# A two-stage attention and expert kernel: every engine's instruction order written out in one table

## The chip, the cores and the metric

One core of one Trainium2 chip. The metric is the device time of the whole kernel in microseconds (us), the median of several runs. The core has a matrix engine (TensorE, PE in the profile), a vector engine (VectorE, DVE), a scalar engine (ScalarE, ACT), GpSimd (POOL) and SyncE (SP). Each engine works through its own list of instructions in order; an instruction waits on semaphores for what others have to finish first. SP and POOL issue nearly all DMA transfers.

## The reference

The first half is a linear recurrence with complex decay over 4 x 768 tokens, 8 heads of 48 channels; the second is four dense experts on its output, all of which every token passes:

```python
for t in range(S):                         # S = 768; the decay a is normalised, magnitude capped at 0.999
    S_re, S_im = ar * S_re - ai * S_im + k_t v_t^T, ar * S_im + ai * S_re
    y[:, :, t] = q_t @ S_re
x = y as 3072 rows of 384
for e in range(4):                         # w1[e] is 384 x 1024, w2[e] is 1024 x 384
    out += p[:, e:e + 1] * (np.maximum(x @ w1[e], 0.0) @ w2[e])      # p: domain_probs, each row divided by its sum
```

All in float32. The kernel writes a float32 operand as a high and a low part (`hi`/`lo`, `hh`/`hl`, `xh`/`xl`) and sums three products of them.

## The kernel before

**Stage 1** (to about 585 us) walks over 12 groups of 256 tokens. For a group `g`, `front()` (L806) makes the decay's running products on DVE and ACT (`norm`, `prefix` at L426 to L429 and L369 to L377, `head`, `tail`), and `attention()` (L706; `near_attention()`, L663, for the first two groups) runs two chunks of 128 tokens: transposes of K (`ktp`, `kp`), the state's increment (`dp`), scores (`sc`, masked on DVE into `scs`, L609) and values (`yp`, copied by ACT into `y`, L632). For the groups from 3 on, `y` goes to DRAM (`y_d`) and comes back transposed as `xa` (L218); groups 0 to 2 are turned on PE (`xp`, L656). ACT and DVE split the result into `xha` (L225) and `xla` (L227). Between these pieces runs `moe1()` on the group before, for experts 0 and 1, in eight steps `f2` per group: `w1_step` makes `ph` (L238), ACT cuts it at zero into `hh` (L249), DVE makes the rest `hl` (L250), and `w2_step` accumulates `po` (L261) from `hh` first and then `hl`. ACT scales `po` into `acc` (L743). `ph3_5` stands for group 3, step 5.

At the start, eight weight tiles are split with help of PE: `lp` (L206, L209), which ACT copies into `wlo` (L210). At the end of stage 1, `check_all()` (L751) reduces some statistics to one number (`n_ps` on PE, L765) and a `flag` (DVE, L766), which SP reads (L1477) to decide if a slower general path is run afterwards; and `late_weights()` (L768) sums weight tiles for stage 2 on DVE (`lws`, `lwt`, L779; `lwl`, `lwm`, L790) and stores them to DRAM (`late_d`, L793, L794). `lw28` is the last of three such batches.

**Stage 2** (to 955.8 us) runs experts 2 and 3 by a fast scheme of matrix products (`pb` and `pob`, L979) on blocks of 384 tokens. Its inputs `Z` are read back from `y_d` (L1118), added up on DVE and POOL (`Z<-Z`), and split into `xh` (ACT, L982) and `xl`. Its tiles take the SBUF space of stage 1, so that the first loads wait for stage 1's last stores. Its weights `shi`, `slo`, `ext` come from `late_d` (L1101, L1102) or from `w` through POOL (L1062, L1066).

The order on each engine is set by the framework's scheduler, which simulates the program, and by what pins it: `behind(ins, prev)` puts one instruction after another of its engine without a semaphore, `tc.keep_in_program_order` keeps an instruction behind the program's earlier ones, `WARM` puts the two last `lp` tiles of the start behind `qp` and `ktp`, and `NPIN` puts a group's scores behind a step of the experts.

Of the kernel before, what the change touches and what calls it, by code (L numbers as in the profile page):

```python
# [121 lines left out]

def fast_path(ctx, tc, qkP, aP, vP, probsP, w, out, flag):
# [1393 lines left out]
```

## Time and profile before

| | us |
|---|---|
| median of 3 runs | 966.08 (965.67 to 966.55) |
| the profiled execution | 963.93 |
| its span in the trace | 962.2 |
| PE busy in it | 935.6 (97%) |
| DVE, ACT, POOL busy | 740.6, 480.2, 165.2 |
| granted TensorE clock, mean | 0.997 of full speed |

The span is the time from the first to the last instruction of the trace; 1.7 us of the execution lie around it. A busy time counts the instructions of an engine; what is left of the span is the time that it waited. The page also names what ended each wait, and follows the chain of work that ended last.

### The profile page before, as it was taken

The numbers are of one execution on the slowest core, as the hardware profiler recorded it, in microseconds if no ns is written. First come the engines' busy times: TensorE is split into PE (matmuls) and PEld (weight loads), VectorE is DVE, ScalarE is ACT, GpSimd is POOL, SyncE is SP. The second block draws the span as 40 slices with busy tenths as digits, with TensorE's granted clock in tenths as the row PEclk, the third lists the DMA queues.
The fourth block names the chain that finished last, engine by engine and source line by source line (L and its number), as shares of the span: only waits on it lengthen the run. The fifth ranks groups of instructions, "written<-read, shape, count | busy, mean of one in ns | idle before, by whom it ended". The sixth has DMA issues, their size and how long they took to land.

```text
span 962.2 us, 18383 instructions
## 1 busy us (share of the span) xinstructions
PE 935.6 (97%) x7037; PEld 912.9 (95%) x7037; DVE 740.6 (77%) x1640; ACT 480.2 (50%) x952; POOL 165.2 (17%) x206
## 2 busy tenths in 40 slices
PE   5899999999999999999999999999999999999997
PEld 3799999989999999999999999999999999999997
DVE  7889989988989999889895676758485757676642
ACT  7756436364464636446253455636454554444430
POOL 6020000000000000000000026333534362322000
PEclk9999999999999999999999999999999999999999
DMA  9686175674857468393949799231514443131112
GB/s 299 193 156 165 54 202 137 166 150 135 179 149 187 120 149 192 113 216 97 215 115 275 268 302 273 60 116 41 151 60 137 155 96 99 50 99 50 50 50 77
DMA packets 131459, 139.57 MB, mean 145 GB/s; under 512 B 8802, under 2 KB 115090, under 8 KB 131362
## 3 DMA queue, kind: packets, MB, share of 16 engines
q1 hardware_dynamic: 116130, 107.84, 38.9%
q0 software_dynamic: 11488, 26.93, 12.1%
q10 hardware_dynamic: 3744, 3.54, 1.4%
q8 instruction: 57, 0.93, 0.4%
q14 instruction: 40, 0.33, 0.1%
HBM read 89.80 MB, written 48.47 MB: 144 GB/s over the span
## 4 chain that ended last, share of the span: by engine, by line
PE 60%; DMA 3%; DVE 2%; ACT 1%; issue 0%; SPq 0%; DVEq 0%; ACTq 0%
PE pob L979 20%; PE pb L979 17%; PE po L261 9%; PE ph L238 9%; PE sc L604 2%; PE yp L621 1%; PE yp L626 1%; DMA RX<-w 1%; PE dp L586 1%; DMA Z<-y_d 1%; PE ktp L567 1%; DMA late_d<-lwl 0%; DMA xa<-y_d 0%; DVE lws L779 0%; DMA y_d<-y 0%
## 5 line engine op out<-in xcount | busy, mean ns | idle before, releaser
L979 PE MATMUL pob<-shi,hid 128*128 128x384 f32 x528 | 148.3, 334 | 0.0
L261 PE MATMUL po<-whi,hh 128*128 128x384 f32 x384 | 129.9, 338 | 1.4 <-ACT hh L249 1.0
L261 PE MATMUL po<-wlo,hh 128*128 128x384 f32 x384 | 128.7, 335 | 0.0
L249 ACT ACTIVATE hh<-ph 128x512 fp32r<-128x512 f32 x96 | 57.1, 595 | 132.0 <-PE ph L238 126.2
L991 POOL TENSOR_TENSOR Z<-Z 128x384 f32<-128x384 f32 x84 | 90.6, 1123 | 112.3 <-DMA Z<-y_d 47.9
L238 PE MATMUL ph<-xha,whi 128*128 128x256 f32 x576 | 103.3, 287 | 2.9 <-ACT xha L225 2.8
L238 PE MATMUL ph<-xla,whi 128*128 128x256 f32 x576 | 101.8, 284 | 0.6 <-DVE xla L227 0.6
L238 PE MATMUL ph<-xha,wlo 128*128 128x256 f32 x576 | 102.4, 284 | 0.0
L979 PE MATMUL pb<-xh,shi 128*128 128x384 f32 x291 | 97.2, 335 | 0.6 <-DVE pb L985 0.6
L979 PEld LDWEIGHTS pob<-shi,hid 128*128 128x128 f32 x528 | 96.4, 188 | 0.2 <-DVE hid L988 0.2
L979 PE MATMUL pb<-xh,slo 128*128 128x384 f32 x288 | 96.2, 334 | 0.0
L979 PE MATMUL pb<-xl,shi 128*128 128x384 f32 x288 | 96.2, 334 | 0.0
L250 DVE SCALAR_TENSOR_TENSOR hl<-ph,hh 128x512 fp32r<-128x512 f32 x96 | 66.0, 688 | 32.3 <-ACT hh L249 31.8
L238 PEld LDWEIGHTS ph<-xha,whi 128*128 128x128 f32 x576 | 85.1, 190 | 5.4 <-ACT xha L225 4.0
L979 PE MATMUL pob<-slo,hid 128*128 128x384 f32 x264 | 88.2, 334 | 0.0
L261 PE MATMUL po<-whi,hl 128*128 128x384 f32 x384 | 84.3, 336 | 0.0
L238 PEld LDWEIGHTS ph<-xla,whi 128*128 128x128 f32 x576 | 83.2, 190 | 1.1 <-DVE xla L227 0.8
L238 PEld LDWEIGHTS ph<-xha,wlo 128*128 128x128 f32 x576 | 82.7, 190 | 0.2 <-issue 0.2
L982 ACT ACTIVATE SN<-pb 128x384 f32<-128x384 f32 x96 | 47.3, 492 | 66.6 <-PE pb L979 59.2
L985 DVE TENSOR_TENSOR xl<-Z,xh 128x384 fp32r<-128x384 f32 x104 | 60.1, 607 | 21.1 <-ACT xh L982 13.3
L261 PEld LDWEIGHTS po<-whi,hh 128*128 128x128 f32 x384 | 72.4, 189 | 2.2 <-ACT hh L249 1.4
L982 ACT ACTIVATE hid<-pb 128x384 fp32r<-128x384 f32 x76 | 37.3, 490 | 72.3 <-PE pb L979 71.7
(227 smaller groups left out, 2069.6 us busy)
## 6 DMA issues: line engine op xcount, KB each, us to landing
qk<-qkP SPq DMA_DIRECT2D x24, 384.0 KB, 3.6
acc_d<-acc POOLq DMA_DIRECT2D x24, 384.0 KB, 4.8
ACC<-acc_d SPq DMA_DIRECT2D x48, 192.0 KB, 2.9
A<-aP SPq DMA_DIRECT2D x22, 384.0 KB, 5.5
k_d<-K SPq DMA_DIRECT2D x40, 192.0 KB, 4.1
Kst<-k_d SPq DMA_DIRECT2D x40, 192.0 KB, 5.7
Z<-y_d SPq DMA_DIRECT2D x16, 384.0 KB, 3.9
q_d<-Q SPq DMA_DIRECT2D x24, 193.5 KB, 3.7
```

Of the source, the lines that this page charges most:

```text
L238: ins = nc.tensor.matmul(ph[:, u, :], wt[:, j * P:(j + 1) * P], xt[:, j, :], start=(n == 0), stop=(n == 3 * NJ - 1))
L249: wts["hh"] = nc.scalar.activation(hh, ph, AF.Relu)
L250: wts["hl"] = nc.vector.scalar_tensor_tensor(hl, ph, 0.0, hh, op0=ALU.max, op1=ALU.subtract)
L261: ins = nc.tensor.matmul(po[t], part[0][:, u, t * P:(t + 1) * P], wts[i][n][:, HD:], start=(i % FE == 0 and part[0] is hh and n == 0), sto ...
L567: ins = nc.tensor.transpose(kt_ps[:, j * P:(j + 1) * P], K[0][:, i, j * CG + c, :], ident)
L586: ins = nc.tensor.matmul(d_ps[o:o + n, h, :], KT[:, h, o:o + n], vc[:, h * D:(h + 1) * D], start=True, stop=True)
L604: ins = nc.tensor.matmul(s_ps[:, h, :], Kc[:, hf * 4 + h, :], Qc[:, hf * 4 + h, :], start=True, stop=True)
L621: ins = nc.tensor.matmul(yo, st[:, o:o + n], Qc[:, o // D, :], start=True, stop=False)
L979: return tc.keep_in_program_order(nc.tensor.matmul(*args, **kw))
L982: return pin(nc.scalar.activation(dst, src, fn, scale=scale))
L985: pin(nc.vector.tensor_tensor(dst, x, y, op=op))
L991: nc.gpsimd.tensor_tensor(dst, x, y, op=op)
```

## The change

The functions compute what they did, with the same instructions on each engine. `behind`, the arguments `prev` that carried its pins, `keep_in_program_order`, `WARM` and `pin` are dropped. A table `ORDER` lists, for each of five engines, runs of indices into that engine's instructions as the program writes them ("116+28" is 28 instructions from number 116 on). `pin_order`, called at the end of the fast path, ties each instruction of an engine to the one before it in the table, so that the scheduler has no choice left. The diff, cut to its core:

```diff
-WARM = {6: "pq", 7: "tk"}
-NPIN = 5
+NSOON = 6
+ORDER = {
+    "PE": (
+        "116+28 0+26 144+4 26+37 64+6 63 70+46 166+16 148+18 182+120 346+30 452+50 302+6 502+8 308+7 510+2 315+31 "
...
+def pin_order(tc, nc):
+    for name, table in ORDER.items():
+        own = [i for i in nc.cur_bb.bb.instructions
+               if i.engine.name == name and type(i).__name__ != "BassTilePoolBoundary"]
+        seq = []
+        for run in table.split():
+            at, _, n = run.partition("+")
+            seq += own[int(at):int(at) + int(n or 1)]
+        for prev, later in zip(seq, seq[1:]):
+            tc.add_manual_dep(later, prev.name,
+                              mybir.DependencyInfo(mybir.DependencyClass.NoSync, mybir.DependencyReason.DATA),
+                              reason="issue order")
...
-    def behind(ins, prev):
...
-                if g == 1:
-                    behind(ln, state["kt", 0, 1])
-                    behind(exp, state["kst", 0, 1])
...
-            if near:
-                wts["hold", g - 1, NF1 // 2 - 2] = ((5, state["sc", g, 1]),)
...
-                    ins = nc.vector.tensor_tensor(*o)
-                    if prev is not None:
-                        behind(ins, prev[1])
+                    nc.vector.tensor_tensor(*o)
...
         def pe(*args, **kw):
-            return tc.keep_in_program_order(nc.tensor.matmul(*args, **kw))
+            return nc.tensor.matmul(*args, **kw)
...
             fast_path(ctx, tc, qkP, aP, vP, probsP, w, out, flag)
+            pin_order(tc, tc.nc)
```

What it moves, at three places. In the rows below the second number of a name is the group (and step, chunk or half), the last one a running number.

**The start, ACT** (group 0, chunk 1). `KT`, `Kst` and `y` are copies that PE waits for; `s1` and `u1` belong to the preparation of group 1. Before:

```order
L568 ACTIVATE KT_156<-ktp0_1_1_408 128x8x48
L400 ACTIVATE s1_488<-s1_488,m2b_89 128x768
L577 ACTIVATE Kst_155<-kp0_1_0_420 112x4x128
L577 ACTIVATE Kst_155<-kp0_1_4_426 112x4x128
L401 ACTIVATE s1_488<-s1_488,lnb_85 128x768
L409 ACTIVATE u1_489<-s1_488 128x768
L411 ACTIVATE u1_489<-s1_488,neg1_83 128x768
L210 ACTIVATE wlo6_569<-lp6_0_571 128x384
L210 ACTIVATE wlo6_569<-lp6_1_575 128x384
L210 ACTIVATE wlo7_580<-lp7_0_582 128x384
L210 ACTIVATE wlo7_580<-lp7_1_586 128x384
L632 ACTIVATE y0_290<-yp0_0_446 112x4x128
```

And now:

```order
L559 ACTIVATE KT_156<-ktp0_1_1_408 128x8x48
L248 ACTIVATE wlo6_569<-lp6_0_571 128x384
L248 ACTIVATE wlo6_569<-lp6_1_575 128x384
L567 ACTIVATE Kst_155<-kp0_1_0_420 112x4x128
L567 ACTIVATE Kst_155<-kp0_1_4_426 112x4x128
L409 ACTIVATE s1_488<-s1_488,m2b_89 128x768
L410 ACTIVATE s1_488<-s1_488,lnb_85 128x768
L415 ACTIVATE u1_489<-s1_488 128x768
L417 ACTIVATE u1_489<-s1_488,neg1_83 128x768
L608 ACTIVATE y0_290<-yp0_0_446 112x4x128
L608 ACTIVATE y0_290<-yp0_1_456 112x4x128
L421 ACTIVATE u1_489,st_w_153<-u1_489,neg1_83 128x768
```

The two `Kst` copies no longer stand behind L400 (now L409), but behind two copies into `wlo6`; the `y` copies stand ahead of `wlo7` and of the last step of `u1`. On PE, the four `lp6` products now stand ahead of `qp`, and the first chunk-1 increment (`dp0_1`) ahead of the first `ph0_0`.

**The middle, PE and DVE.** On PE, before, the second half of group 3's values (`yp3_1`) stands behind the whole step `ph2_6`:

```order
L604 MATMUL sc3_1_1_2251<-Qst_154,Kst_155 128x128 x4
L238 MATMUL ph2_6_2382<-xha2_1826,wlo12_766 128x256 x3
L567 MATMUL ktp3_1_0_2258<-wide_76,K3_1851 128x128 x3
L238 MATMUL ph2_6_2382<-xla2_1827,whi12_600 128x256 x2
L567 MATMUL ktp3_1_1_2263<-wide_76,K3_1851 128x128 x3
L238 MATMUL ph2_6_2382<-xla2_1827,whi12_600 128x256
L238 MATMUL ph2_6_2382<-xha2_1826,whi13_602 128x256 x3
L238 MATMUL ph2_6_2382<-xha2_1826,wlo13_769 128x256 x3
L238 MATMUL ph2_6_2382<-xla2_1827,whi13_602 128x256 x2
L621 MATMUL yp3_1_2314<-Qst_154,G3_0_2238 48x128 x2
```

And now behind a part of `ph2_5` and three products of `po2_4`:

```order
L588 MATMUL sc3_1_1_2251<-Qst_154,Kst_155 128x128 x4
L558 MATMUL ktp3_1_0_2258<-wide_76,K3_1851 128x128 x3
L558 MATMUL ktp3_1_1_2263<-wide_76,K3_1851 128x128 x3
L271 MATMUL ph2_5_2279<-xha2_1826,whi11_598 128x256
L271 MATMUL ph2_5_2279<-xha2_1826,wlo11_706 128x256 x3
L271 MATMUL ph2_5_2279<-xla2_1827,whi11_598 128x256 x3
L286 MATMUL po2_4_0_2208<-whi8_592,hh2_4_2188 128x384
L286 MATMUL po2_4_0_2208<-wlo8_618,hh2_4_2188 128x384
L286 MATMUL po2_4_1_2209<-whi8_592,hh2_4_2188 128x384
L602 MATMUL yp3_1_2314<-Qst_154,G3_0_2238 48x128 x2
```

It stands one step (`ph` and `po`) earlier. On DVE, around 300 us, `pf7` and `sk7` are the running products of group 7, `hl5_3` and `scs6` what PE waits for. Before:

```order
L426 TENSOR_TENSOR pf7_4_3637<-A7_3047 128x384
L250 SCALAR_TENSOR_TENSOR hl5_3_3768<-ph5_3_3748,hh5_3_3767 128x512
L428 TENSOR_TENSOR A7_3047<-pf7_4_3637 128x96
L429 TENSOR_TENSOR A7_3047<-pf7_4_3637 128x96
L426 TENSOR_TENSOR pf7_5_3641<-A7_3047 128x384
L428 TENSOR_TENSOR A7_3047<-pf7_5_3641 128x96
L429 TENSOR_TENSOR A7_3047<-pf7_5_3641 128x96
L609 TENSOR_TENSOR scs6_0_0_3803<-sc6_0_0_3798,maskp_142 128x512
```

And now:

```order
L386 TENSOR_TENSOR sk7_16a_3743<-A7_3047 128x2x48
L387 TENSOR_TENSOR sk7_16a_3743<-A7_3047 128x2x48
L393 TENSOR_TENSOR A7_3047<-sk7_16a_3743 128x3x16
L394 TENSOR_TENSOR A7_3047<-sk7_16a_3743 128x3x16
L277 SCALAR_TENSOR_TENSOR hl5_3_3768<-ph5_3_3748,hh5_3_3767 128x512
L591 TENSOR_TENSOR scs6_0_0_3803<-sc6_0_0_3798,maskp_142 128x512
L591 TENSOR_TENSOR scs6_0_1_3810<-sc6_0_1_3805,maskp_142 128x512
```

31 instructions of group 7, from the rest of `pf7_4` to `sk7_16a`, have moved ahead of `hl5_3`.

**The passage to stage 2, DVE and ACT.** DVE before, with the last batch of late weights done ahead of the flag:

```order
L779 TENSOR_TENSOR lws28_6834<-lws28_6834 128x128 x2
L227 TENSOR_TENSOR xla11_6694<-xa11_6621,xha11_6693 128x768
L790 TENSOR_TENSOR lwl28_6837<-lws28_6834,lwh28_6836 128x768 x2
L250 SCALAR_TENSOR_TENSOR hl10_7_6717<-ph10_7_6697,hh10_7_6716 128x512
L766 TENSOR_SCALAR flag_58<-n_ps_6744 1x1
L250 SCALAR_TENSOR_TENSOR hl11_0_6890<-ph11_0_6870,hh11_0_6889 128x512
```

And now, with nine instructions of that batch behind the flag:

```order
L277 SCALAR_TENSOR_TENSOR hl10_7_6717<-ph10_7_6697,hh10_7_6716 128x512
L734 TENSOR_SCALAR flag_58<-n_ps_6744 1x1
L747 TENSOR_TENSOR lws28_6834<-lws28_6834 128x128
L747 TENSOR_TENSOR lwt28_6835<-lw28_6829 128x128 x2
L754 TENSOR_TENSOR lwm28_6838<-lw28_6829,lwt28_6835 128x256
L754 TENSOR_TENSOR lwm28_6838<-lw28_6829,lwt28_6835 128x128
L754 TENSOR_TENSOR lwm28_6838<-lw28_6829,lwt28_6835 128x256
L754 TENSOR_TENSOR lwl28_6837<-lws28_6834,lwh28_6836 128x768 x2
L754 TENSOR_TENSOR lwm28_6838<-lwt28_6835 128x384
L277 SCALAR_TENSOR_TENSOR hl11_0_6890<-ph11_0_6870,hh11_0_6889 128x512
```

On SP, the four stores of that batch to `late_d` now follow the read of the flag; they stood ahead of it. ACT, `hh` being what PE's `po` waits for and `xh` the first inputs of stage 2, before:

```order
L982 ACTIVATE xh10_7219<-Z_7195 128x384
L249 ACTIVATE hh11_2_6965<-ph11_2_6946 128x512
L982 ACTIVATE xh15_7229<-Z_7195 128x384
L982 ACTIVATE xh4_7207<-Z_7195 128x384
L982 ACTIVATE xh1_7201<-Z_7195 128x384
L982 ACTIVATE xh11_7221<-Z_7195 128x384
L982 ACTIVATE xh13_7225<-Z_7195 128x384
L982 ACTIVATE xh14_7227<-Z_7195 128x384
L249 ACTIVATE hh11_3_7000<-ph11_3_6981 128x512
```

And now:

```order
L276 ACTIVATE hh11_2_6965<-ph11_2_6946 128x512
L938 ACTIVATE xh9_7217<-Z_7195 128x384
L938 ACTIVATE xh6_7211<-Z_7195 128x384
L938 ACTIVATE xh1_7201<-Z_7195 128x384
L938 ACTIVATE xh7_7213<-Z_7195 128x384
L938 ACTIVATE xh14_7227<-Z_7195 128x384
L938 ACTIVATE xh10_7219<-Z_7195 128x384
L276 ACTIVATE hh11_3_7000<-ph11_3_6981 128x512
L276 ACTIVATE hh11_4_7035<-ph11_4_7016 128x512
```

`hh11_3` now stands behind `xh10`, which needs the fifth of DVE's sums of `Z`. Behind it ten more `xh` and the first `slo3` (from `shi3`, which POOL loads) stand ahead of `hh11_6`, and `shi5` and `shi6` ahead of the copy of the first `pb`; on POOL, the store of `acc11_0` stands ahead of the loads of `shi3` and `shi4`. From the third unit of stage 2 on the order is nearly the same as before.

## Rows read from the trace of the kernel before

**Rows 1.** The page: busy time (share of the span) and instructions of each engine.

```profile
PE 935.6 (97%) x7037; PEld 912.9 (95%) x7037; DVE 740.6 (77%) x1640; ACT 480.2 (50%) x952; POOL 165.2 (17%) x206
```

**Rows 2.** Busy time of each engine by stretch: the stretch's ends, its length, then PE, weight loads, DVE, ACT, POOL (us and number of instructions), the granted clock, the DMA engines' busy share and GB/s.

```profile
0.00:48.00 48.00, 33.51 (x235) 25.04 (x236) 37.53 (x105) 36.66 (x71) 15.60 (x34) 0.96 0.76 247
28.00:30.00 2.00, 2.00 (x22) 1.98 (x19) 2.00 (x7) 0.39 (x2) 0.00 (x0) 0.50 0.83 290
30.00:32.00 2.00, 2.00 (x17) 1.67 (x14) 2.00 (x6) 0.71 (x2) 0.00 (x0) 0.68 0.01 3
48.00:384.00 336.00, 331.37 (x2947) 322.36 (x2946) 302.83 (x700) 171.15 (x314) 17.03 (x22) 1.00 0.62 153
384.00:553.00 169.00, 169.00 (x1512) 165.50 (x1511) 136.73 (x332) 78.49 (x148) 4.85 (x7) 1.00 0.67 186
553.00:601.00 48.00, 47.16 (x308) 46.27 (x307) 33.45 (x73) 28.04 (x60) 21.89 (x28) 1.00 0.98 288
601.00:940.00 339.00, 338.82 (x1954) 338.27 (x1953) 224.50 (x422) 164.50 (x359) 105.81 (x116) 1.00 0.29 86
940.00:962.20 22.20, 15.76 (x91) 15.44 (x90) 5.56 (x11) 1.40 (x3) 0.00 (x0) 0.94 0.27 84
```

**Rows 3.** What PE waited for: us in total, times, the longest.

```profile
PE lp L206 <- DMA wst<-w: 9.3, 1, 9.3
PE ph L238 <- ACT xha L225: 2.8, 3, 1.6
PE po L261 <- ACT hh L249: 1.0, 2, 0.7
```

**Rows 4.** The timelines of PE and of ACT from 27 to 51 us: start, duration, the instructions, and the idle time before with what ended it.

```profile
27.16 4.52 PE L457 MATMUL qp<-Q,wide 128*64 128x128 f32 x40 [2.81 <-DVE Q L497]
42.05 2.05 PE L604 MATMUL sc<-Qst,Kst 112*128 112x128 f32 x16 [0.64 <-ACT Kst L577]
47.16 2.92 PE L656 MATMUL xp<-y,band 112*128 112x128 f32 x24 [0.28 <-ACT y L632]
50.65 0.62 PE L238 MATMUL ph<-xha,whi 128*128 128x256 f32 x3 [0.58 <-ACT xha L225]
...
40.57 0.94 ACT L400 ACTIVATE s<-s,m2b 128x768 f32<-128x768 f32 x1 [0.34 <-DVE st_m L391]
41.42 1.06 ACT L577 ACTIVATE Kst<-kp 112x512 f32<-112x512 f32 x2
44.91 1.61 ACT L210 ACTIVATE wlo<-lp 128x384 fp32r<-128x384 f32 x4
```

**Rows 5.** The timeline of PE at 102 and at 194 us.

```profile
102.28 0.62 PE L238 MATMUL ph<-xha,whi 128*128 128x256 f32 x3 [0.58 <-ACT xha L225]
194.27 0.62 PE L238 MATMUL ph<-xha,whi 128*128 128x256 f32 x3 [1.59 <-ACT xha L225]
```

**Rows 6.** The timelines of DVE and PE at 301 to 312 us: `hl5_3`, the last of the 31 moved instructions, and PE's first use of `hl5_3`.

```profile
301.35 0.69 DVE L250 SCALAR_TENSOR_TENSOR hl<-ph,hh 128x512 fp32r<-128x512 f32 x1 [0.44 <-ACT hh L249]
311.40 0.20 DVE L377 TENSOR_TENSOR A<-sk_16a 128x48 f32<-128x48 f32 x1
307.97 0.87 PE L261 MATMUL po<-whi,hl 128*128 128x384 f32 x4
```

**Rows 7.** The timeline of DVE from 542 to 565 us.

```profile
542.62 0.69 DVE L779 TENSOR_TENSOR lwt<-lw 128x128 f32<-128x128 f32 x3
543.23 0.96 DVE L790 TENSOR_TENSOR lwm<-lw,lwt 128x256 fp32r<-128x256 f32 x3
544.77 0.55 DVE L790 TENSOR_TENSOR lwm<-lwt 128x384 fp32r<-128x384 f32 x1
547.72 1.82 DVE L790 TENSOR_TENSOR lwl<-lws,lwh 128x768 fp32r<-128x768 f32 x2
550.65 0.15 DVE L766 TENSOR_SCALAR flag<-n_ps 1x1 int32<-1x1 f32 x1 [0.51 <-PE n_ps L765]
563.61 1.50 DVE L985 TENSOR_TENSOR Z<-Z 128x384 f32<-128x384 f32 x3 [1.24 <-DMA Z<-y_d]
```

**Rows 8.** The chain that ended last, at 549 us and at 556 us (start, us, what), then what the DMA engines moved from 541 to 570 us in 40 equal slices of 0.725 us.

```profile
549.57 4.29 DMA late_d<-lwl
556.33 7.19 DMA Z<-y_d
...
GB/s 7 0 82 360 100 362 362 350 362 34 212 398 398 424 424 288 25 0 0 189 205 242 334 283 203 132 250 225 223 346 384 407 413 411 411 424 392 348 369 384
```

**Rows 9.** The timelines of ACT, PE and POOL from 566 to 584 us, and the median landing time of POOL's loads of `shi`.

```profile
567.11 0.58 ACT L249 ACTIVATE hh<-ph 128x512 fp32r<-128x512 f32 x1
581.78 0.85 ACT L982 ACTIVATE shi<-Z 128x768 fp32r<-128x768 f32 x1 [0.35 <-DVE Z L985]
569.72 0.34 PE L261 MATMUL po<-whi,hh 128*128 128x384 f32 x1
574.61 0.44 PE L261 MATMUL po<-whi,hh 128*128 128x384 f32 x1 [0.44 <-ACT acc L743]
583.17 0.34 PE L261 MATMUL po<-whi,hh 128*128 128x384 f32 x1
575.32 0.56 POOL L745 DMA_DIRECT2D acc_d<-acc  x1
shi<-w POOLq DMA_DIRECT2D x6, 192.0 KB, 6.6
```

More of the change, by code (lines that the diff above doesn't have):

```diff
@@ L260, in w2_step @@
                     for n in part[1]:
-                        ins = nc.tensor.matmul(po[t], part[0][:, u, t * P:(t + 1) * P], wts[i][n][:, HD:],
-                                               start=(i % FE == 0 and part[0] is hh and n == 0),
-                                               stop=(i % FE == FE - 1 and part[0] is hl))
-                        for k0, prev in hold:
-                            if k >= k0:
-                                behind(ins, prev)
-                        k += 1
+                        nc.tensor.matmul(po[t], part[0][:, u, t * P:(t + 1) * P], wts[i][n][:, HD:],
+                                         start=(i % FE == 0 and part[0] is hh and n == 0),
+                                         stop=(i % FE == FE - 1 and part[0] is hl))
     class MoE:
@@ L603, in scores @@
                     for h in range(4):
-                        ins = nc.tensor.matmul(s_ps[:, h, :], Kc[:, hf * 4 + h, :], Qc[:, hf * 4 + h, :],
-                                               start=True, stop=True)
-                        if h == 0 and prev is not None:
-                            behind(ins, prev)
+                        nc.tensor.matmul(s_ps[:, h, :], Kc[:, hf * 4 + h, :], Qc[:, hf * 4 + h, :],
+                                         start=True, stop=True)
                     s_sb = small.tile([P, 4, C], F32, tag="sc", name=f"scs{g}_{c}_{hf}", bufs=4)
@@ L655, in turn_x @@
                     o = HOFF - (2 * D * p - P * j)
-                    ins = nc.tensor.matmul(xp[:, j, :], band[:, o:o + P], y[:, p, c * C:(c + 1) * C],
-                                           start=(p == ps[0]), stop=(p == ps[-1]))
-                    if g == 0 and c == 0 and p == ps[0]:
-                        behind(ins, state["yl", g, 1])
-            last["xp"] = ins
+                    nc.tensor.matmul(xp[:, j, :], band[:, o:o + P], y[:, p, c * C:(c + 1) * C],
+                                     start=(p == ps[0]), stop=(p == ps[-1]))
             return slice(c * C, (c + 1) * C), xp
@@ L747, in done @@
                     nc.gpsimd.dma_start(acc_d[g], acc, accum_op=ALU.add)
[L748 removed]
+            mo.block(g, xh, xl, 0, NF1, done, between)
         def check_all():
@@ L838, in front @@
                     yield 2.7
-                last["dve"] = tail(1, CG)
+                tail(1, CG)
                 yield 2.7
@@ L861, in front @@
                 yield None
-                last["dve"] = tail(0, CG)
+                tail(0, CG)
                 yield 4.8
@@ L890, in stream @@
                 if g > NSEL:
-                    here = nc.sync.dma_start(here_d, Kst[0:1, 0, CG - 1, 0:1])
-                    behind(here, last["q"])
-                    last["q"] = here
-                qk = load_qk(g, last["q"])
+                    nc.sync.dma_start(here_d, Kst[0:1, 0, CG - 1, 0:1])
+                qk = load_qk(g)
                 if g + 1 < NG:
-                    A.append(load_a(g + 1, prev=last["q"]))
+                    A.append(load_a(g + 1))
                 for r in front(g, A[g], qk):
```

297 lines of the change are left out of this document (116 added, 181 removed), and 23 rows, old and new, of the table ORDER.

## The prediction, made before the changed kernel ran

> **What bounds the kernel now.** I read the busy times first: PE works 935.6 of 962.2 us [rows 1], so a new order can win at most the 26.6 us in which PE idles, and it does not shorten PE's own work. The table by stretch says where they lie [rows 2]: 14.5 us before 48 us, 4.6 us from 48 to 384 us, nothing from 384 to 553 us, 0.8 us at the passage to stage 2 (553 to 601 us), 0.2 us after that, and 6.4 us at the end. The list of PE's waits says what ended them: 9.3 us are the first weight load [rows 3], which the order of instructions cannot bring earlier, and 2.8 us the first `Q` from DVE [rows 4]. The tail after the last matmul is left as it is. So what an order can win is some 2 us at the start, 4.6 us in the middle, 0.8 us at the passage, and whatever the half clock costs at 28 to 32 us. DVE, with 302.8 of 336 us busy from 48 to 384 us [rows 2], has little room there: an order that brings one DVE instruction forward puts another one back. The question is therefore as much which new waits the table makes. The profiled execution took 963.93 us against a median of 966.08; I work out differences in its trace and set them on the median. A difference of 0.2%, 1.9 us, is about what a measurement here can tell from no change.
>
> **The start: -1.3 us.** After `qp`, three waits of PE hang on ACT: 0.64 us for `Kst`, 0.28 us for `y`, 0.58 us for `xha` [rows 4]. ACT was free at 40.23 us, idled 0.34 us for DVE before L400, ran it from 40.57 us, and began `Kst` at 41.42 us [rows 4]; now only two `wlo` copies of 0.40 us (four took 1.61) stand ahead of `Kst`, so it begins at 41.03 us, 0.4 us earlier. `y` stood behind four `wlo` copies, 1.61 us, of which two are now behind it: its wait goes. `dp0_1` on PE fills the 0.58 us. Sum 0.4 + 0.3 + 0.6 = 1.3 us. The 2.81 us wait before `qp` [rows 4] becomes shorter, as `lp6` fills about half of it, but `qp` still starts when `Q` comes, at 27.16 us, and what `lp6` took afterwards only turns into a wait for `K`. There is one danger. After the idle 2.81 us the granted clock fell to 0.50 at 28 to 30 us, the 1.2 GHz level, and was 0.68 at 30 to 32 us [rows 2]; those 4 us cost PE 2.0 x 0.50 + 2.0 x 0.32 = 1.6 us of work, hidden today because PE had to wait for `K` anyway. If the idle moves behind `qp`, the clock may be low for the transposes that are not hidden. So the bounds are a loss of 0.3 us and a gain of 2 us.
>
> **The middle: -2.2 us.** The largest wait is 1.59 us at 194.27 us for `xha` of group 3 [rows 5], the first group that goes through DRAM. With `yp3_1` one step earlier on PE (4.2 us), `y` is stored and read back earlier by that much, and the wait goes. The 0.58 us at 102.28 us [rows 5] is of the same kind, one ACT step with DVE work brought forward before it; I count it as gone. The others (1.0 us for `hh`, 0.6 us more for `xha`, and the rest of the 4.6) I leave. Against it stands DVE at 300 us. `hl5_3` was done at 302.04 us and PE wanted it at 307.97 us [rows 6], a slack of 5.9 us. The 31 instructions now ahead of it end with the one at 311.40 us; between 301.96 us and 311.60 us they are all of DVE's work but two `scs`, one `hl` (2.0 us) and 0.6 us of idle, so 7.0 us. The 0.44 us that DVE idled before `hl5_3` is used up by them. That leaves it 5.9 + 0.44 - 7.0 = 0.7 us late. I take that as covered, for ahead of this place the table fills other short idle stretches of DVE; if it is not, similar places follow up to 340 us and I bound their sum by three times this one, 2.1 us. So the middle lies between a gain of 4.6 us (all idle gone) and a loss of 2.1 us; I take 1.59 + 0.58 = 2.2 us of gain, the two waits with a row and a reason.
>
> **The passage to stage 2: +2.5 us.** Here I expect a new wait, and it comes from the flag. DVE's flag waits for `n_ps` on PE, 550.65 us [rows 7]. What now stands behind it takes, by the same instructions of the same batch before: `lws` 0.2, two `lwt` 0.4, three `lwm` 0.96, two `lwl` 1.82, one `lwm` 0.55 [rows 7], 3.9 us from 550.8 us, so the last store can be issued at about 554.9 us, where it was at 549.57 us [rows 8]. SP too waits for the flag before the first of the four stores. By their size, 2.6 MB at the 0.40 to 0.42 MB/us that the DMA engines moved when they were full [rows 8], they need 6.4 us from some 551.3 us on, so they cannot be done before 557.7 us; with the 4.29 us that the last one took before [rows 8], 559.2 us instead of 553.86 us. The first loads of stage 2 use the same memory and stand behind it on SP. The second of DVE's waits for `Z` ended at 563.61 us [rows 7]; 4.9 us later (5.3 less one load that moved back behind them) is 568.5 us. Four sums at 0.47 us each follow (three took 1.50), then `xh10`, 0.5 us, and only then `hh11_3`, 0.5 us: 571.4 us. Before, `hh11_3` was done at 567.69 us [rows 9], and PE's `po11_3` takes it at 569.72 us [rows 9]. So PE waits 1.7 us. The 0.44 us wait for `acc` at 574.61 us [rows 9] lies in its shadow and goes. Two smaller items follow. `shi5` and `shi6`, 0.85 us each [rows 9], stand ahead of the copy of the first `pb`, which nothing covers for long: 0 to 1.7 us, I take half, 0.8 us. And `hh11_6` waits for `slo3`, which waits for POOL's `shi3`, whose load is issued only after the store of `acc11_0`, at about 576.8 us by its place before (575.32 us [rows 9]) and the wait above; 6.6 us to landing [rows 9] and two ACT copies make 584.3 us, where PE wants `hh11_6` at 583.17 us [rows 9] plus the wait of 1.3 us, 584.5 us. If that load takes two microseconds more it costs 1.8 us; I put 0.4 us. Sum 1.7 - 0.4 + 0.8 + 0.4 = 2.5 us. If the four loads of `Z`, alone on the queue, land 2 us sooner, the first term is nothing: +0.4 us. If the stores land at 560.5 us, it is 3.0 us, with the other items at their upper ends +6.1 us.
>
> The Trainium skill, page "DMA: Bandwidth & Descriptors", section "Specifications", gives about 358 GB/s as the limit of one core's share of the HBM. The slices of the trace show up to 424 GB/s [rows 8], so the measurement decides. By the page's figure the stores would need an estimated 7.3 us, and the first term would be 0.9 us longer.
>
> **Stage 2 and the end: nothing.** PE's list there is the same but for a few swaps, and it idles 0.2 us in 339 us [rows 2].
>
> The sum is -1.3 - 2.2 + 2.5 = -1.0 us: 962.9 us for an execution like the profiled one, 965.1 us on the median.
>
> **The rivals.** *The passage is hidden (faster).* The rows leave room: `Z` needs to land 2 us sooner than I reckon, and with 0.98 of the DMA engines' time busy there [rows 2] the later start of the stores may also free the wires for them. If in addition the middle loses 3.5 of its 4.6 us, the sum is -1.3 - 3.5 + 0.4 = -4.4 us: 961.7 us. Against it speaks that DVE can start `Z` only after the flag's chain.
>
> *The wait for `hh11_3` halves the clock (slower).* One mechanism: late flag, late stores, late `Z`, late `xh10`, and PE idle before `po11_3` for about as long as before `qp`. After 2.81 us idle there the clock fell to 0.50 [rows 4, 2], after 1.59 us in the middle it did not (1.00 from 48 to 384 us [rows 2]). [...] With a wait of 3.0 us and 1.6 us lost to the half clock, the passage costs 3.0 - 0.4 + 0.8 + 0.4 + 1.6 = 5.4 us; with nothing won in the middle, since DVE's lateness at 300 us eats the two waits, the sum is -1.3 + 5.4 = +4.1 us: 970.2 us.
>
> The Trainium skill, page "TensorE: Matmul & The Clock Gate", Part 1, says that TensorE's clock falls back to half whenever the engine has been idle for some microseconds, and recovers under load. The trace agrees at 28 us (0.50 after 2.81 us of idle).
>
> *The table does not take effect.* The listed order shows that it does, with about a quarter of PE's rows moved, so I give this no chance of its own.
>
> **How the numbers follow.** The forecast (965.1 us, between 964.2 and 968.0 us) gets 0.38, the faster rival 0.36, the slower one 0.26; so faster by over 0.2% 0.36, the same 0.38, slower 0.26. The middle's full gain of 4.6 us and the passage at +0.4 us would be -5.5 us, 960.6 us; the slower rival gives 970.2 us. I cut a little off both: 960.8 to 970.0 us. The likeliest case alone would hold from 963.5 to 967.5 us.
>
> **What would show it.** Right: no wait over 0.3 us for `xha` near 190 us; the last store to `late_d` landing at 558 to 560 us; a wait of PE for `hh` of 1 to 2.5 us near 566 to 572 us; PE's idle time from 48 to 384 us at 2 to 3 us. The start is right if PE reaches the first `ph0_0` 1 us or more earlier than at 50.65 us. Wrong: new waits for `hl` or `scs` near 300 to 340 us, which would make the middle a loss; a granted clock below 1.00 after 560 us, which is the slower rival; or no wait at all at `po11_3`, which is the faster one.

## The result, and the profile after

The changed kernel takes 979.51 us (978.19 to 980.79, 4 runs), the kernel before 966.03 us (965.67 to 966.55, 4 runs) beside it: a ratio of 1.0139, interval 1.0120 to 1.0158. The forecast was 965.1 us with a range up to 970.0 us; the change makes the kernel slower by 13.5 us. The profiled execution took 978.19 us, its span is 976.5 us, 14.3 us more than before.

First the page's row of busy times (engine, us, share of the span, instructions), to be read against [rows 1]:

```profile
PE 937.8 (96%) x7037; PEld 912.4 (93%) x7037; DVE 757.1 (78%) x1640; ACT 482.3 (49%) x952; POOL 168.8 (17%) x206
```

The same number of instructions on each engine. PE is busy 2.2 us longer and idle 38.7 instead of 26.6 us; 12.1 of the 14.3 us are added waiting. What PE waited for (us in total, times, the longest), against [rows 3]:

```profile
PE lp L246 <- DMA wst<-w: 7.5, 1, 7.5
PE dp L575 <- DMA v<-vP: 5.9, 1, 5.9
PE yp L605 <- DMA v<-vP: 4.4, 3, 3.2
PE pb L935 <- DVE pb L941: 3.1, 7, 0.5
...
PE sc L588 <- DMA Qst<-q_d: 2.5, 2, 1.7
PE ktp L558 <- DVE K L517: 2.2, 1, 2.2
PE po L286 <- ACT hh L276: 0.8, 1, 0.8
```

Before, no wait of PE after the first weights was longer than 2.81 us, and the list had none for `v`. Now loads stand at the top: `v`, the values of a chunk, and `Qst`; and there is a small wait seven times over for `pb`, in stage 2. The timeline of PE at the two longest, and at the wait that I had forecast for the passage (start, duration, instructions, idle time before with what ended it):

```profile
134.94 1.94 PE L575 MATMUL dp<-v,KT 128*64 128x48 f32 x32 [5.91 <-DMA v<-vP]
...
189.74 0.43 PE L605 MATMUL yp<-scs,v 128*48 128x128 f32 x4 [3.21 <-DMA v<-vP]
...
579.89 0.44 PE L286 MATMUL po<-whi,hh 128*128 128x384 f32 x1 [0.80 <-ACT hh L276]
```

The table by stretch (columns as in [rows 2]): the long stretch of stage 1, and four of 4 us around 134.94 us.

```profile
48.00:384.00 336.00, 322.46 (x2876) 314.03 (x2876) 302.10 (x688) 169.70 (x309) 16.14 (x21) 0.99 0.61 148
128.00:132.00 4.00, 1.03 (x6) 0.71 (x5) 3.75 (x8) 0.00 (x0) 0.00 (x0) 1.00 1.01 343
132.00:136.00 4.00, 1.06 (x22) 1.06 (x23) 0.43 (x2) 0.00 (x0) 0.00 (x0) 0.64 1.16 257
136.00:140.00 4.00, 4.00 (x31) 3.91 (x28) 1.24 (x2) 0.69 (x2) 0.00 (x0) 0.50 0.20 33
140.00:144.00 4.00, 4.00 (x34) 3.75 (x35) 3.43 (x10) 0.60 (x1) 0.00 (x0) 1.00 0.00 0
```

From 48 to 384 us PE now idles 13.5 us where it idled 4.6 [rows 2]. While it stood from 129.0 to 134.9 us its granted clock went to 0.50, the 1.2 GHz level, and stayed there to 140 us: the 16 `sc` products behind the wait took 3.54 us; 16 of them took 2.05 us at 42.05 us before [rows 4].

Where on the way the time is lost shows when the start of one and the same matmul is compared in the two traces. The table takes the first `ph` of some groups, two of the `pb` and the last matmul, and gives the difference to the profiled execution of the kernel before, in us, for this kernel and for the experiments that follow (e1 to e11).

```
start of                 ph1_0   ph2_0   ph3_0  ph10_0  ph11_0  1st pb  97th pb  last
before, at us           102.28  149.37  194.27  507.68  550.54  585.26   612.74  955.42
after                    -1.75   +5.94   +8.15   +8.60   +9.21   +9.70    +9.53  +14.03
e1 before as table       -0.15   -0.14   -0.64   +0.06   +0.06   +1.01    +1.02   +0.99
e2 SP of before          -0.84   -1.44   +2.68   +1.57  +26.33  +32.22   +32.09  +36.59
e3 v ahead               -0.86   +5.18   +5.61   +6.61   +7.44   +8.27    +8.12  +12.71
e4 POOL of before        -1.87   +5.91   +5.50   +4.52   +5.13   +5.30    +4.54   +3.84
e5 small loads first     -0.54   -0.40   +0.31   +1.22   +1.83   +2.29    +2.18   +6.71
e6 mended                -0.87   -0.76   +2.19   +1.13   +1.75   +2.46    +1.70   +1.04
e7 new start only        -2.38   -0.12   +0.27   +2.34   +2.34   +1.64    +1.64   +1.48
e8 passage only          +0.00   +0.99   +0.99   +0.88   +1.50   +2.46    +2.31   +3.29
e9 big loads first       -0.12   +9.16   +9.07   +9.79   +9.79   +9.22    +9.23   +9.21
e10 after again          -1.15   +6.92  +11.22  +11.73  +12.34  +12.46   +12.32  +16.83
e11 mended stage 1       -1.02   -0.73   -0.09   -0.73   +4.14   +6.27    +6.27   +6.07
```

In the row "after": 1.75 us won by group 1, 7.7 us lost up to `ph2_0`, 2.2 us more up to `ph3_0`, 1.1 us on the 350 us to `ph11_0`, 0.3 us at the passage (to the 97th `pb`), 4.5 us in stage 2, and 0.2 us behind the last matmul: 14.3 us, rounded.

**Group 2: four big loads on SP's queue.** SP's timeline from 122 us on, after (start, duration of the issue, transfer):

```profile
122.24 1.81 SPq L530 DMA_DIRECT2D Kst<-k_d  x2
124.14 0.55 SPq L530 DMA_DIRECT2D Qst<-q_d  x1
124.75 0.94 SPq L366 DMA_DIRECT2D qk<-qkP  x2
125.72 0.91 SPq L359 DMA_DIRECT2D A<-aP  x2
126.67 1.12 SPq L549 DMA_DIRECT2D v<-vP  x2
128.08 0.33 SPq L530 DMA_DIRECT2D Qst<-q_d  x1
129.25 1.19 SPq L530 DMA_DIRECT2D Kst<-k_d  x2
```

And before, from 97 us on:

```profile
97.11 2.09 SPq L558 DMA_DIRECT2D v<-vP  x2
...
127.69 1.19 SPq L533 DMA_DIRECT2D Qst<-q_d  x2
128.92 0.98 SPq L533 DMA_DIRECT2D Kst<-k_d  x2
134.33 0.28 SPq L891 DMA_DIRECT2D here_d<-Kst  x1
134.65 0.84 SPq L347 DMA_DIRECT2D qk<-qkP  x2
135.53 0.91 SPq L338 DMA_DIRECT2D A<-aP  x2
```

Before, group 2's `v` was asked for 34 us ahead of its use (at 131.31 us); the inputs `qk` and `A` of group 3 (four loads of 384 KB) were pinned behind the last of group 2's `Qst` and `Kst`, by the small store to `here_d`. Without that pin they stand ahead of `v` and of the rest of `Qst` and `Kst`. The page's row of `v` loads (KB each, median us from issue to landing) was

```profile
v<-vP SPq DMA_DIRECT2D x24, 192.0 KB, 2.4
```

and is now

```profile
v<-vP SPq DMA_DIRECT2D x24, 192.0 KB, 6.2
```

The two that PE stood for took 8.22 and 8.43 us by the chain that ended last after (start, us, what), both behind `qk` and `A` in the queue:

```profile
126.67 8.22 DMA v<-vP
...
181.18 8.43 DMA v<-vP
```

**Stage 2: POOL's sums.** One unit of it, after; POOL's timeline, then DVE's:

```profile
663.77 8.46 POOL L947 TENSOR_TENSOR Z<-Z 128x384 f32<-128x384 f32 x7 [7.35 <-DVE xl L944]
...
667.76 2.65 DVE L941 TENSOR_TENSOR xl<-Z,xh 128x384 fp32r<-128x384 f32 x2
670.33 0.55 DVE L941 TENSOR_TENSOR pb<-pb,SN 128x384 f32<-128x384 f32 x1
```

And the same unit before:

```profile
650.68 2.11 POOL L991 TENSOR_TENSOR Z<-Z 128x384 f32<-128x384 f32 x2 [4.30 <-DVE xl L985]
653.73 3.54 POOL L991 TENSOR_TENSOR Z<-Z 128x384 f32<-128x384 f32 x3 [0.94 <-DVE xl L988]
657.82 1.20 POOL L991 TENSOR_TENSOR Z<-Z 128x384 f32<-128x384 f32 x1 [0.56 <-DVE xl L988]
...
657.60 1.84 DVE L985 TENSOR_TENSOR xl<-Z,xh 128x384 fp32r<-128x384 f32 x2
```

A unit is some 23 us of stage 2. Before, POOL made six sums of `Z` per unit; now five and seven in turn. The seven run on while DVE makes two more `xl`, 1.3 us each beside them, and the pair takes 0.8 us longer; DVE's sum for `pb` stands behind it, and PE waits 0.46 us for that. It does so in six of the seven units with seven sums (626.01 to 903.43 us); in the other one it waits 0.44 us for `hid`.

### The profile page after: what moved, and what is told of

It is laid out like the page before. It is cut to its first block, busy times and chain, and to the rows that moved or that the text cites. A ratio compares the mean times of both kernels' runs of the same rounds, so it can differ in the third digit from the quotient of the medians.

```text
span 976.5 us, 18366 instructions
## 1 busy us (share of the span) xinstructions
PE 937.8 (96%) x7037; PEld 912.4 (93%) x7037; DVE 757.1 (78%) x1640; ACT 482.3 (49%) x952; POOL 168.8 (17%) x206
## 3 DMA queue, kind: packets, MB, share of 16 engines
q10 hardware_dynamic: 3744, 3.54, 1.5%
## 4 chain that ended last, share of the span: by engine, by line
PE 74%; DVE 10%; DMA 7%; ACT 4%; issue 2%; SPq 1%; ACTq 0%; DVEq 0%
PE pob L935 18%; PE pb L935 15%; PE ph L271 15%; PE po L286 15%; PE sc L588 4%; DMA v<-vP 3%; PE yp L605 2%; PE dp L575 2%; PE yp L602 1%; DVE xl L941 1%; DMA Kst<-k_d 1%; DMA q_d<-Q 1%; PE ktp L558 1%; DMA k_d<-K 1%; DMA Qst<-q_d 1%
## 5 line engine op out<-in xcount | busy, mean ns | idle before, releaser
L947 POOL TENSOR_TENSOR Z<-Z 128x384 f32<-128x384 f32 x84 | 93.9, 1146 | 119.7 <-DVE xl L944 60.9
L271 PE MATMUL ph<-xha,whi 128*128 128x256 f32 x576 | 103.6, 287 | 0.6 <-ACT xha L260 0.6
L271 PE MATMUL ph<-xha,wlo 128*128 128x256 f32 x576 | 100.4, 282 | 0.0
L941 DVE TENSOR_TENSOR xl<-Z,xh 128x384 fp32r<-128x384 f32 x104 | 65.1, 660 | 20.9 <-ACT xh L938 12.0
```

What stands on the lines that cost most here:

```text
L271: nc.tensor.matmul(ph[:, u, :], wt[:, j * P:(j + 1) * P], xt[:, j, :], start=(n == 0), stop=(n == 3 * NJ - 1))
L941: nc.vector.tensor_tensor(dst, x, y, op=op)
L947: nc.gpsimd.tensor_tensor(dst, x, y, op=op)
```

## The experiments

The theory: the loads on SP's queue in stage 1 cost some 10 us, POOL's order in stage 2 some 4, the rest cancels. Rivals: that the table itself costs (the ties between instructions); that PE's, DVE's or ACT's new order is the loss and the loads come late because of it; that another execution would be without the loss. In all the experiments the change's code is kept, and only what its table lists is altered; where a diff below shows rows, they are SP's issues in order, a name's first number being the chunk (0 or 1) where there are two, and the last a running number. Line numbers differ from kernel to kernel.

**e1: the table with the order of before.**

```diff
 def pin_order(tc, nc):          # kept as the change has it
-ORDER = the change's five lists
+ORDER = five lists that give the order in which before runs
```

> The changed kernel's code, with a table that holds the order of the kernel before on all five engines. Theory A (the time comes from the order in the table, above all that of SP's loads): 966 us, as before, within 1 us. Rival (the chain of ordering ties or the dropped scheduler itself costs something, whatever the order): over 968 us.

Measured: 964.87 us (10 runs) against 963.94; ratio 1.0003 (0.9994 to 1.0013). The table and its ties cost nothing; the loss lies in the order that it writes down.

**e2: SP's list of before, the other four of the change.**

```diff
 ORDER["PE"], ["DVE"], ["ACT"], ["POOL"]   # of the change
-ORDER["SP"] of the change
+ORDER["SP"] that gives the order of before
```

> The changed table with SP's list alone put back to the order of before. Theory A (PE waits for v, 5.9 + 3.2 + 1.0 us, and for Qst, 1.7 us, because SP issues those loads later): 979.5 - 11.8 = 967.7 us, between 966 and 970; no wait of PE for v near 135 and 190 us. Rival B (DVE's running products ahead of scs and hl are what is late, and take over once the loads are early): 974 to 979 us, with PE waiting for DVE in the same places.

Measured: 1001.0 us, ratio 1.0373 (1.0348 to 1.0398). Up to `ph10_0` the waits for `v` are gone and 7.0 us are won over the change (+1.57 for +8.60), as expected, though a wait of 3.50 us comes in at 170.13 us; as a whole the expectation missed by 33 us. PE's waits in its trace:

```profile
PE sc L590 <- DMA Kst<-k_d: 16.7, 1, 16.7
```

and SP's timeline ahead of it, at 502 us:

```profile
502.04 2.26 SPq L527 DMA_DIRECT2D q_d<-Q  x4
526.05 0.33 SPq L760 DMA_DIRECT2D late_d<-lwt  x1
526.43 1.33 SPq L532 DMA_DIRECT2D Qst<-q_d  x2
527.87 2.49 SPq L527 DMA_DIRECT2D k_d<-K  x4
```

SP stands from 504.3 to 526.05 us at the store of a late weight (`lwt`), whose copy ACT makes only at 525.5 us in the change's order; the stores of `K`, the loads of `Kst` and so `sc` of group 11 are queued behind it. Here the list of one engine does not go with the lists of the others.

**e3: the change, with `v` ahead of the big loads** in groups 2 and 3.

```diff
 Qst<-q_d_1_1379 (first half)
+v_0_1590<-vP
+v_1_1592<-vP
 qk_1527<-qkP x2
 A_1530<-aP x2
-v_0_1590<-vP
-v_1_1592<-vP
 Qst<-q_d_1_1379 (second half)
...
+v_1_2106<-vP
 qk_2000<-qkP x2
 A_2003<-aP x2
-v_1_2106<-vP
```

> The changed table with only five of SP's rows shifted: the loads of v2 go ahead of the four loads of qk3 and A4 (1.5 MB), and that of v3_1 ahead of those of qk4 and A5. Theory A in its narrow form (what holds v back is the four big loads just ahead of it in the queue): waits of 5.9 and 3.2 us gone, 970.4 us, between 969 and 972. Rival C (v is late because its place is behind the group's round trips of q and k; two places forward do little): 975 us or more, with a wait of over 3 us left at 135 us.

Measured: 973.13 us, ratio 1.0084 (1.0067 to 1.0101). The wait for `v` falls from 5.91 to 0.58 us, but a new one appears:

```profile
PE po L286 <- ACT hh L276: 4.0, 2, 2.9
```

ACT's timeline shows why:

```profile
137.94 0.21 ACT L539 ACTIVATE TB<-Qst 48x8 f32<-48x8 f32 x1 [10.01 <-DMA Qst<-q_d]
138.07 1.05 ACT L276 ACTIVATE hh<-ph 128x512 fp32r<-128x512 f32 x2
```

The second half of `Qst` is still behind the 1.5 MB, ACT stands 10 us for it, and `hh1_6` is queued behind that little copy (before, the copies from this `Qst` stood behind the copy of `y`). With the 2.9 us idle the clock is at half as well (0.50 from 138 to 144 us). So `v` is not the only load that the big ones hold up; two waits lay one over the other.

**e4: the change with POOL's list of before.**

```diff
-ORDER["POOL"] of the change
+ORDER["POOL"] that gives the order of before
```

> The changed table with POOL's list alone put back to the order of before. Theory D (in stage 2 the change loses 4 us, 0.75 us per unit, because POOL's sums of Z now run in one stretch of 8.5 us beside DVE's xl, which take 1.3 us each instead of 0.55): 975.5 us, with no wait of 0.46 us for DVE's pb in stage 2. Rival E (the order on DVE and ACT in stage 2 makes that loss): 979.5 us, the waits stay.

Measured: 973.66 us (968.14 to 978.61), ratio 1.0113 (1.0078 to 1.0148). From the first to the last matmul of stage 2 the change lost 4.3 us on before (+9.70 to +14.03); this one wins 1.5 (+5.30 to +3.84), and the list of its waits holds none for `pb`, while `PE dp L578 <- DMA v<-vP` is there as in the change, with 6.2 us. The term of stage 2 is POOL's order. PE's list there is the same in both traces, and each of the seven waits of the change moves what follows by 0.7 us, 5.2 us in all: more than the 3.2 us of idle time (e4 is 0.7 us ahead of before on this stretch, which leaves the 4.5 us). The spread of the four runs is wide, and more on that is in e10.

**e5: the change with all small loads first**: `qk` and `A` back behind `here_d`.

```diff
 Qst<-q_d_1_1379 (first half)
-qk_1527<-qkP x2
-A_1530<-aP x2
 v_0_1590<-vP
 v_1_1592<-vP
 Qst<-q_d_1_1379 (second half)
 Kst<-k_d_1_1468 x2
 here_d<-Kst
+qk_1527<-qkP x2
+A_1530<-aP x2
...
+v_1_2106<-vP
 qk_2000<-qkP x2
 A_2003<-aP x2
-v_1_2106<-vP
```

> The changed table with seven of SP's rows shifted: the four big loads qk3 and A4 go behind the small loads of group 2 (v2, the second half of Qst, Kst), as before, and v3_1 goes ahead of qk4 and A5. After run e3, in which v2 was early and ACT's copy TB then waited for the second half of Qst with hh1_6 behind it, theory A in its wider form: the big loads hold back all of group 2's small ones, and PE's idle halves the clock on top. Then PE has no wait over 0.7 us from 125 to 145 us and a clock of 1.00 there, 5.9 + 3.4 us are won, and 3.2 us at 190 us: 12 us less than the changed kernel, a ratio to before of 1.001 to 1.004. Rival F (the early TB copy on ACT is what counts, whenever Qst comes): a wait of 2 to 3 us for hh near 137 us stays, ratio 1.007 or more.

Measured: 971.3 us, ratio 1.0057 (1.0037 to 1.0077). `ph2_0` starts 0.40 us earlier than before instead of 5.94 us later: the whole 6.3 us come back. `v` is asked for at 125.99 us here, as late as in the change (126.67 us), but with nothing big ahead of it, and PE waits 0.65 us for it: what cost the 5.91 us are the big loads ahead, not the late request alone. The ratio is above the 1.001 to 1.004 expected. What PE still waits for:

```profile
PE pb L935 <- DVE pb L941: 3.1, 7, 0.5
PE ktp L558 <- DVE K L517: 2.2, 1, 2.2
PE sc L588 <- DMA v<-vP: 1.8, 1, 1.8
PE yp L605 <- DMA v<-vP: 1.7, 1, 1.7
```

Two waits of 1.7 to 1.8 us at 169 and 348 us, and stage 2's 4.4 us. The first stands ahead of `sc`, which reads `Qst` and `Kst` and not `v`, the load that the profile names; which load it was is not shown.

**e6: everything mended that had been found**: e5, POOL's list of before, `q_d` ahead of `k_d` in group 3, and `v` ahead of `qk` and `A` in group 7.

```diff
 here_d<-Kst
 qk_1527<-qkP x2
 A_1530<-aP x2
+q_d_0_1843<-Q x2
+q_d_1_1846<-Q x2
 k_d_0_1892<-K x2
-q_d_0_1843<-Q x2
...
+v_0_4280<-vP
+v_1_4282<-vP
 qk_4172<-qkP x2
 A_4175<-aP x2
-v_0_4280<-vP
-v_1_4282<-vP
```

> As e5, and besides SP sends q of group 3 ahead of its k and loads v7 ahead of qk8 and A9, and POOL's list is that of before. Theory A with D: also the waits of 1.7 us at 175 us and 1.0 us at 355 us go, and the 4 us of stage 2: ratio 0.996 (0.994 to 0.998), faster than before by what the new start wins and the old middle lost. Rival G (the other lists, on PE, ACT and DVE, lose time of their own in the middle): ratio 1.000 or more.

Measured: 964.05 us (961.08 to 969.87, 11 runs) against 964.74; ratio 1.0001 (0.9984 to 1.0017). All of the loss is gone, and nothing is won: the expectation missed. What e6 wins over e5 is POOL's list; at `ph10_0` the two stand at +1.13 and +1.22 us. In the profiled execution the first chunk of group 3 waits for its `Qst`,

```profile
PE sc L591 <- DMA Qst<-q_d: 2.6, 1, 2.6
```

and the clock falls to 0.61 at 168 to 172 us; that gives back 3.0 us from `ph2_0` to `ph3_0`. I did not find the place in the queue at which group 3 waits for none of `Qst`, `Kst` and `v`.

**e7: only the start of the change** (what was issued before 103 us), the order of before after it.

```diff
-ORDER, all five lists, of the change
+ORDER: of the change up to 103 us, then of before
```

> The order of before, but all that started before 103 us in its trace stands in the order of the change, on all five engines. The prediction's term for the start was -1.3 us; the trace of the changed kernel shows -1.75 us there. Theory: ratio 0.9982 (0.997 to 0.999). Rival (the gain is given back, as group 2 then waits for DVE anyway): 1.000.

Measured: 965.2 us, ratio 1.0009 (1.0000 to 1.0018). `ph1_0` starts 2.38 us earlier, `ph1_4` only 0.08 us earlier:

```profile
PE ph L306 <- DVE xla L296: 2.7, 2, 2.0
```

PE is sooner at `xla` (103.6 us) than DVE has it ready. That place is right at the joint of the two orders, so the wait may be the joint's; what e7 shows is that the gain does not last with the order of before behind it; in the changed kernel `ph1_4` stays 1.74 us ahead. The rival's 1.000 is the one that fits.

**e8: only the passage** (what was issued from 505 to 612 us), the order of before around it.

```diff
-ORDER, all five lists, of the change
+ORDER: of before, between 505 and 612 us of the change
```

> The order of before, but what started between 505 and 612 us stands in the order of the change: the flag ahead of nine DVE instructions of the last late weights, SP's stores behind the flag, hh11_3 behind xh10. The prediction's term: +2.5 us, ratio 1.0026. From the trace of the changed kernel: a wait of 0.8 us for hh11_3 in place of those of 0.44 and 0.41 us, so +0.5 to 1 us: ratio 1.0005 to 1.001.

Measured: 967.19 us, ratio 1.0030 (1.0018 to 1.0042), so +2.9 us (1.7 to 4.1); my term was +2.5. In the trace 0.88 us are lost by `ph10_0`, ahead of all that was changed, and 2.41 us from there to the last matmul. PE waits 1.28 us at 572.7 us, where I had put 1.7 us at 569.7 us:

```profile
PE po L318 <- ACT hh L308: 2.2, 3, 1.3
```

**e9: only the big loads first, in the order of before.** The theory's core alone; PE, DVE, ACT and POOL as before.

```diff
-v_0_1590<-vP
-v_1_1592<-vP
 y_d_100<-y_837 x2
...
-Qst<-q_d_1_1379 x2
-Kst<-k_d_1_1468 x2
-here_d<-Kst
+Qst<-q_d_1_1379 (first half)
 qk_1527<-qkP x2
 A_1530<-aP x2
+v_0_1590<-vP
+v_1_1592<-vP
+Qst<-q_d_1_1379 (second half)
+Kst<-k_d_1_1468 x2
+here_d<-Kst
```

> The order of before, with one thing of the change on SP: qk3, A4 (four loads, 1.5 MB) and then v2 stand ahead of the second half of group 2's Qst and of Kst, and so far later for v2 than before (97 us). Theory A: PE waits 4 to 6 us for v2 near 135 us and the clock is at half for some us behind it, so 6 to 9 us slower, ratio 1.006 to 1.010. Rival (in the order of before, PE has other work there, and the loss comes only together with the other lists): ratio under 1.003.

Measured: 973.6 us (972.76 to 974.61), ratio 1.0092 (1.0077 to 1.0106): +8.8 us from a few rows of one list. PE's wait, and the table by stretch behind it:

```profile
PE dp L613 <- DMA v<-vP: 7.0, 1, 7.0
```

```profile
136.00:140.00 4.00, 1.76 (x23) 1.48 (x24) 0.00 (x0) 0.00 (x0) 0.00 (x0) 0.56 1.17 253
140.00:144.00 4.00, 4.00 (x34) 3.79 (x31) 2.02 (x5) 0.00 (x0) 0.00 (x0) 0.58 0.28 41
```

6.98 us of idle, and from 138.2 to 144 us some 2.5 us for the low clock (1.8 x 0.44 + 4 x 0.42); `ph2_0` is 9.16 us late, and the later columns stay between 9.07 and 9.79. No slack behind it takes any of it up.

**e10: the change once more**, unaltered, with more runs.

```diff
 # no edit
```

> The changed kernel once more, beside the others on one chip: ratio 1.014 (1.012 to 1.016). Theory on its spread: where the waits of 5.9 and 3.2 us come out a little shorter, the clock is at half for less time, so runs with a higher granted clock are the shorter ones.

Measured: 979.15 us (976.59 to 984.79, 6 runs), ratio 1.0150 (1.0124 to 1.0176). The runs of the changed order spread over 8 us, and the mean granted clock follows them only in part (0.991 at 977.47 us, 0.994 at 981.50 us, 0.990 at 984.79 us), so that a slower clock alone does not explain it. The traces show where most of the difference comes in: up to `ph2_0` the executions of the change, of e4 and of this one agree within 1 us (+5.94, +5.91, +6.92), at `ph3_0` they stand at +8.15, +5.50 and +11.22, though SP's list is the same in all three. PE's wait ahead of the second `yp` of group 3 was 3.21, 0.91 and 3.54 us there, the last with a clock of 0.57 at 192 to 196 us. (The profile puts that last one down to an instruction of DVE's that `yp` does not read; `v` was asked for at 183.12 us; with the 8.22 to 8.43 us of the two loads above it would land at 191.3 to 191.6 us, and the wait ended at 191.25 us. So I take it for a wait for `v`, which the profile does not show.) That the other runs spread for the same reason was not shown.

**e11: e6 up to 505 us, before from there on.**

```diff
-ORDER, all five lists, of the change
+ORDER: of e6 up to 505 us, then of before
```

> Up to 505 us (of before's trace) the changed order with SP's rows mended as in e6, and Qst of group 3 also ahead of its k; from there on, passage and stage 2, the order of before. Theory: e6 lost 2.6 us at 169 us to that Qst and 1 us at the passage; without them the ratio is 0.997 (0.995 to 0.999), and this version beats both. Rival (another wait comes up in the place of the one for Qst, as DVE is near its limit there): 0.9995 or more.

Measured: 968.46 us, ratio 1.0029 (1.0017 to 1.0040). Stage 1 is 0.73 us ahead of before at `ph10_0`; at the joint a wait comes in,

```profile
PE po L294 <- ACT hh L284: 2.9, 1, 2.9
```

at 512.2 us, with a clock of 0.69 behind it, and 1.4 us for `acc` at 580.9 us. The version that should have beaten both does not; no kernel tried here is faster than before.

## Why the prediction was wrong, point by point

**The step that failed** is one that the sum does not have: SP's queue in stage 1. I took "what an order can win" and what it can lose in the middle from PE, ACT and DVE alone, looked at SP only at the passage, and wrote "the middle: -2.2 us" with the loss bounded by DVE's lateness at 300 us. My remark that the question is which new waits the table makes was right; I looked for them on the wrong engine. e9 shows the missing term by itself: +8.8 us (7.4 to 10.2) for one group, since four loads of 384 KB went ahead of loads that PE needed next; e5 shows it from the other side. The pins listed as dropped were the sign: whatever a dropped pin held back can now come early, and a load that comes early delays those behind it. The rest of the middle, 2.2 us up to `ph3_0`, is waits of 1.67 us for `Qst` and 3.21 us for `v` in place of the 1.59 us for `xha`. The second is of the same kind: it is gone in e3 and e5, where the second `v` stands ahead of `qk` and `A`. The first I had put down to `k_d` ahead of `q_d`; but e6, which turns these round, still waits 2.61 us there, so its cause stays open.

**The middle's two waits.** The 1.59 us for `xha` near 194 us [rows 5] went, also in e6 and e11 without the long waits, as the earlier `yp3_1` should do; the 0.58 us at 102.28 us [rows 5] stayed (0.58 us at 100.53 us). Yet no gain is left of it: e11, with the loads mended, is no further ahead at `ph10_0` (-0.73) than at `ph1_0` (-1.02); it still waits 1.87 us for `Kst` at 168.35 us, with a clock of 0.60 from 168 to 172 us. DVE's lateness at 300 us did not show: one wait of 0.43 us at 315.9 us, put down to `acc`, and none to `hl` or `scs` from 300 to 340 us (the `scs` that PE used next was done at 315.58 us, 0.3 us before that wait ended). That bound was too wide.

**The start, -1.3 us.** The sum held: measured -1.75 us at `ph1_0` (-1.15 in e10). PE came to `ph0_0` only 0.55 us earlier than at 50.65 us, not the 1 us that I wanted to see: that sign left out that the 1.1 us of `dp0_1` now lie ahead of it. The 2.24 us wait for `K` is what `lp6` ahead of `qp` turned into, as said. In the profiled execution of the change the clock was 1.00 behind it. But the danger that I named did come: behind the same wait of 2.24 us the mean clock from 32 to 36 us was 0.57 to 0.64 in e2, e3, e5, e6, e10 and e11, and these stood only 0.54 to 1.15 us ahead at `ph1_0`, against 1.75 to 2.38 us in the change, e4 and e7, where it stayed at 1.00. So -1.3 us lies between two cases, and which one comes varies from run to run (the change and e10 are the same kernel). e7 adds what the term left out: with the order of before behind it the gain is given back in a wait of 2.03 us for DVE at 103.6 us.

**The passage, +2.5 us.** The mechanism is there: the last store to `late_d` is issued at 564.84 us and SP goes on at 569.10 us, 559.9 us when the 9.2 us of delay are taken off (I had 559.2); `hh11_3` stands behind `xh10`; PE waits 0.80 us for it (1.7 forecast, 1.28 in e8), and the 0.44 us for `acc` [rows 9] is gone. In the change it is worth 0.3 us up to the 97th `pb`, alone +2.9 us (2.4 us in e8's trace behind `ph10_0`), part of which are waits of 0.46 us for `pb` and 0.31 us for `hid` early in stage 2. In its place in the change the size was too large: the wait for `hh11_3` is 0.9 us shorter than reckoned (DVE's second wait for `Z` ends at 576.71 us, 567.5 us without the delay, where I had 568.5), and the two items for `shi5`, `shi6` and `hh11_6` show as no more than one wait of 0.33 us at 609.67 us, where before there was one of 0.41 us at 600.12 us.

**Stage 2, nothing.** Wrong by 4.5 us. I read it from PE's list ("the same but for a few swaps") and never compared POOL's, whose grouping of sums changed in each unit and held up DVE's `xl`. e4 shows it: without that list the loss is gone.

**The rivals.** The one on the slow side (a wait halves the clock) has the mechanism right and the place wrong: not `hh11_3` at the passage, where the wait was 0.80 us and the clock 1.00, but `v` at 134.9 us, with 5.91 us. The one on the fast side had the passage nearly right (+0.4 us, measured 0.3), and the middle wrong. That the table costs nothing by itself, which I did not price, e1 shows (1.0003).

## What to carry to other kernels

When pins are dropped, list for every one of them what it held back, and follow each queue as closely as the bounding engine: a load that may start earlier is a cost to every smaller load behind it that is wanted sooner. Compare the lists of all engines in every stage, also where the bounding engine's own list is the same. And where PE is busy without slack, a wait of microseconds is paid in full to the end, with the low clock on top; and an order is one thing over all engines: parts of two put together may be worse than either, as in e2.

## What the runs showed of the hardware

**The length of a wait did not decide alone if the clock fell.** The plainest case is one and the same wait: PE stood 2.24 us for `K` near 32 us in nine traces, and the mean clock from 32 to 36 us was 1.00 in three of them (after, e4, e7) and 0.57 to 0.64 in six (e2, e3, e5, e6, e10, e11). Behind waits of 3.02 us (27.1 us, e1), 2.03 us (103.6 us, e7) and 3.21 us (189.7 us, after) PE's granted clock stayed 1.00 too; behind 1.84 us (168.8 us, e5: 0.71), 2.61 us (169.2 us, e6: 0.61), 2.93 us (138.7 us, e3: 0.50) and 3.54 us (191.3 us, e10: 0.57 from 192 to 196 us) it fell. So the two rows that my slower rival set side by side, a fall behind 2.81 us and none behind 1.59 us, do not tell what a wait in between does.

**One kind of DVE operation is slow beside POOL's sums, another not.** `xl<-Z,xh` took 1.3 us beside them (2.65 us for two at 667.76 us) and 0.55 us at its median in the stage, while the sum `pb<-pb,SN` of the same size at 670.33 us, under POOL's row of the same time, took 0.55 us. POOL's sums were slower as well: 1.21 us each here (seven in 8.46 us), 0.98 us in a unit of before in which no `xl` ran beside them (six in 5.86 us, at 631.76 us).
The Trainium skill, page "SBUF — State Buffer", section "SBUF: two separate sides", states why that can be: a DVE operation with two inputs in SBUF and GpSimd's share a pair of ports, which one holds for a whole instruction. The rows agree: `xl` reads two tiles that other engines prepared in SBUF and is held up, the sum that reads `pb`, PE's own output, is not.
